# A gated linear-attention kernel with a rational MLP: its token groups split in two halves, each half's 64 rows of v stacked with the running state

## The chip, the cores and the metric

The kernel runs on one core of one Trainium2 chip. The metric is the device time of one execution in microseconds. Three runs of the kernel before gave 537.37, 537.48 and 537.78; the median is 537.48.

## The reference, cut to what matters

There are 4 batches x 8 heads, 768 tokens, head size 48. Attention is a recurrence along the tokens, and its output feeds an MLP whose activation is a quotient of polynomials:

```python
for t in range(S):
    state = alpha[:, :, t, :, None] * state + np.einsum('bhd,bhe->bhde', k[:, :, t], v[:, :, t])
    y[:, :, t] = np.einsum('bhd,bhde->bhe', q[:, :, t], state)
x = y.transpose(0, 2, 1, 3).reshape(3072, 384)
h = x @ w_in                                   # 384 -> 2048
P = a[0] + a[1]*h + a[2]*h**2 + a[3]*h**3
Q = 1 + abs(b[0])*abs(h) + abs(b[1])*h**2
out = (P / (Q + 1e-6)) @ w_out                 # 2048 -> 384
```

The weights, `a` and `b` come as 64-bit floats; the kernel joins the two words of each weight into one 32-bit float on the chip.

## The kernel before, in words

**Groups.** The 3072 tokens are cut into 24 *groups* of 128 tokens, 0 to 23, six for each batch. Within a group the recurrence is done in matrix form. Products of alpha towards the group's end (`suffix`) and from its start (`prefix`) are two scans on VectorE; k is multiplied by the one (`mult_k`), q by the other (`mult_q`), mostly on GpSimd. Of the 128 partitions, each pair of heads holds the first head's 48 dimensions in rows 0 to 47 and the second's in rows 64 to 111.

Then TensorE makes the scores k.q of the group (`sc_mm`, L505: 8 products of 128 columns, K = 48, two heads at a time in the two halves of the rows). ScalarE copies all eight heads' scores out (`sc_evac`), GpSimd zeroes the part above the diagonal (`sc_mask`). TensorE turns k into rows of tokens (`k_turn`, L523) and ScalarE copies that (`k_evac`). `attn_mm` holds three sorts of products: state times q (L547, 12 products of 128 columns and 32 output rows), v times scores (L547, 16 of the same shape), and k times v for the next state (L566, 16 products of 48 columns and 32 output rows). A 32-bit product is two records in the trace, so these are 16 records of L505, 24 + 32 of L547 and 32 of L566. `decay` (GpSimd) multiplies the state by the group's total of alpha, which `totals` makes; `kv_add` (VectorE) adds the new part. The first group of a batch (0, 6, 12, 18) has no state products, the last (5, 11, 17, 23) has no turn of k and no new state.

`x_hi` (ScalarE) and `x_lo` (VectorE) copy the group's output as a sum of two shorter floats for the MLP.

**Units.** The MLP is 96 *units* of 512 hidden values x tokens. Units 0 to 9 are plain 32-bit products (L643, L656). Units 10 to 95 are *wide*: 9 products of 512 columns in (L670) and 9 out (L689; L683 in the last super-block of tokens), with ten elementwise steps between on ScalarE, VectorE and GpSimd (t1, ah, q1, qm, t2, t3, ars, sq, p, t, g, gh, gl). Sixteen units use the tokens of four groups.

**What sets the order.** Every step is an `add` call with its engine, its prerequisites and sometimes a second engine (`alt`). A list packed into the string `ORDER` says in which order the steps are issued and which of them go to their second engine. Each engine runs its own steps strictly in that order. All DMAs of inputs go through SyncE's one queue in that order too; `raw_qk[0]` is the only buffer for k and q of groups 4 to 23, so the loads of group g wait for the transpose `tqk` of group g - 1.

**PSUM.** Scores take banks 4 and 5, the turned k then bank 4, the output y bank 4, the new state part bank 5. The constant that the scans read as a floor lies from group 4 on in bank 5, where every group's scores overwrite it: `set_floor` writes it again for each group, and the scores of group g have to wait for `prefix` of g + 1.

**Start.** `prime` is a small ScalarE instruction (function Copy) and stands late in the order.

## Time and profile before

| | |
|---|---|
| profiled execution, its own time | 537.53 us (span 535.8) |
| median of the runs | 537.48 us (537.37 to 537.78) |
| TensorE busy | 517.1 us, 97% |
| VectorE busy | 480.7 us, 90%, 716 instructions |
| ScalarE busy | 430.2 us, 80%, 730 instructions |
| GpSimd busy | 392.4 us, 73%, 387 instructions |
| DMA | 57.46 MB, 107 GB/s on average |

Busy time is the time in which at least one of the engine's instructions was under way. An instruction of VectorE or ScalarE is recorded a little longer than it holds the engine: the next one starts before the record ends. Engines are abbreviated PE (TensorE), PEld (its weight loads), DVE (VectorE), ACT (ScalarE), POOL (GpSimd), SPq (SyncE's DMA queue).

Three stretches are used below: the opening up to 129.7 us, where wide unit 16 begins; the middle up to 455.2 us, where unit 80 begins; and the close up to 535.8 us. Units are counted by nine L670 records each from the first at 93.99 us.

### The profile page before, as it was taken

The numbers are of one execution on the slowest core, as the hardware profiler recorded it, in microseconds if no ns is written. First come the engines' busy times: TensorE is split into PE (matmuls) and PEld (weight loads), VectorE is DVE, ScalarE is ACT, GpSimd is POOL, SyncE is SP. The second block draws the span as 40 slices with busy tenths as digits, with TensorE's granted clock in tenths as the row PEclk, the third lists the DMA queues.
The fourth block names the chain that finished last, engine by engine and source line by source line (L and its number), as shares of the span: only waits on it lengthen the run. The fifth ranks groups of instructions, "written<-read, shape, count | busy, mean of one in ns | idle before, by whom it ended". The sixth has DMA issues, their size and how long they took to land.

```text
span 535.8 us, 11861 instructions
## 1 busy us (share of the span) xinstructions
PE 517.1 (97%) x4342; PEld 428.1 (80%) x4342; DVE 480.7 (90%) x716; ACT 430.2 (80%) x730; POOL 392.4 (73%) x387
## 2 busy tenths in 40 slices
PE   8878997999999999999999999999999999999996
PEld 7777886888788788888778878878888887889986
DVE  3998988999998999999979989999999997898885
ACT  3699988899988977788868777777778876787983
POOL 2436557697998988996676888759888765687673
PEclk9999999999999999999999999999999999999999
DMA  9988875454555353545324524342632341020301
GB/s 246 260 249 219 214 229 116 116 140 113 128 140 117 92 127 71 104 96 109 92 68 87 112 73 94 97 87 59 128 95 55 88 83 18 1 40 1 59 1 62
DMA packets 146174, 57.46 MB, mean 107 GB/s; under 512 B 133056, under 2 KB 138688, under 8 KB 146112
## 3 DMA queue, kind: packets, MB, share of 16 engines
q1 hardware_dynamic: 145824, 56.27, 43.7%
q8 instruction: 35, 0.57, 0.5%
q10 hardware_dynamic: 288, 0.39, 0.2%
q14 instruction: 27, 0.22, 0.1%
HBM read 47.98 MB, written 4.72 MB: 98 GB/s over the span
## 4 chain that ended last, share of the span: by engine, by line
PE 70%; SPq 7%; DMA 7%; DVE 6%; POOL 4%; ACT 3%; issue 2%; DVEq 0%; POOLq 0%; ACTq 0%
PE ps L670 29%; PE ps L689 23%; PE ps L683 6%; PE ps L547 5%; SPq L402 4%; PE ps L505 3%; DMA wo_words<-in_moe_w_out_dram 2%; DMA raw_a<-in_alpha_dram 2%; PE ps L656 1%; SPq L409 1%; DMA tv<-in_v_dram 1%; POOL gh_gl L778 1%; PE ps L523 1%; PE ps L566 1%; DVE t L748 1%
## 5 line engine op out<-in xcount | busy, mean ns | idle before, releaser
L670 PE MATMUL ps<-x,wi 128*128 128x512 f32 x774 | 209.1, 396 | 3.7 <-DVE t L771 3.7
L689 PE MATMUL ps<-gh_gl,wo 128*128 128x512 f32 x630 | 176.5, 400 | 0.1
L670 PEld LDWEIGHTS ps<-x,wi 128*128 128x128 f32 x774 | 143.8, 188 | 36.1 <-ACT ah L725 3.0
L737 POOL TENSOR_TENSOR qm<-qm,ah 128x512 f32<-128x512 f32 x96 | 124.2, 1295 | 24.7 <-ACT qm L734 14.7
L689 PEld LDWEIGHTS ps<-gh_gl,wo 128*128 128x128 f32 x630 | 115.5, 188 | 27.6 <-DVE parts L704 0.5
L778 POOL TENSOR_TENSOR gh_gl<-t,gh_gl 128x512 fp32r<-128x512 f32 x74 | 96.2, 1301 | 16.4 <-ACT gh_gl L774 6.3
L728 ACT ACTIVATE t<-ps,coef 128x512 f32<-128x512 f32 x96 | 74.5, 776 | 21.2 <-PE ps L670 12.8
L755 ACT ACTIVATE ps<-qm,one_eps 128x512 f32<-128x512 f32 x96 | 66.3, 691 | 20.5 <-POOL qm L737 11.9
L732 POOL TENSOR_SCALAR qm<-ah,bab 128x512 f32<-128x512 f32 x62 | 47.8, 771 | 47.4 <-ACT ah L725 22.5
L762 DVE SCALAR_TENSOR_TENSOR t<-t,coef,ps 128x512 f32<-128x512 f32 x96 | 71.0, 739 | 12.6 <-ACT ps L758 11.7
L748 DVE TENSOR_TENSOR t<-t,ps 128x512 f32<-128x512 f32 x96 | 65.1, 678 | 11.3 <-ACT t L728 5.6
L752 DVE SCALAR_TENSOR_TENSOR t<-t,coef,ps 128x512 f32<-128x512 f32 x96 | 71.3, 744 | 2.5 <-ACT ah L725 0.7
L725 ACT ACTIVATE ah<-ps 128x512 f32<-128x512 f32 x96 | 57.0, 593 | 17.7 <-PE ps L670 12.0
L771 DVE SCALAR_TENSOR_TENSOR t<-ps,t 128x512 f32<-128x512 f32 x96 | 66.1, 688 | 1.9
L765 DVE SCALAR_TENSOR_TENSOR ps<-qm,ps 128x512 f32<-128x512 f32 x96 | 66.0, 688 | 0.0
L774 ACT ACTIVATE gh_gl<-t 128x512 fp32r<-128x512 f32 x86 | 53.7, 628 | 9.2 <-DVE t L771 7.3
L758 ACT ACTIVATE ps<-ps 128x512 f32<-128x512 f32 x96 | 56.1, 585 | 2.0
L488 POOL TENSOR_TENSOR tqk<-tqk,tg 128x512 f32<-128x512 f32 x21 | 27.2, 1294 | 13.4 <-DVE tg L461 7.7
L491 POOL TENSOR_TENSOR tqk<-tqk,fp 128x512 f32<-128x512 f32 x21 | 27.2, 1295 | 12.6 <-DVE wo_words L274 5.0
L516 POOL TENSOR_SCALAR_AFFINE_SELECT sc<-sc 128x1024 f32<-128x1024 f32 x24 | 26.2, 1092 | 13.2 <-ACT sc L512 4.0
L461 DVE TENSOR_TENSOR_SCAN tg<-ta,ps 128x528 f32<-128x528 f32 x24 | 29.8, 1244 | 6.5 <-ACT ta L445 6.5
L683 PE MATMUL ps<-wo,gh_gl 128*128 128x384 f32 x180 | 35.5, 337 | 0.0
(117 smaller groups left out, 723.0 us busy)
## 6 DMA issues: line engine op xcount, KB each, us to landing
raw_a<-in_alpha_dram SPq DMA_DIRECT2D x160, 48.0 KB, 2.1
raw_qk<-in_k_dram SPq DMA_DIRECT2D x160, 48.0 KB, 2.1
raw_qk<-in_q_dram SPq DMA_DIRECT2D x160, 48.0 KB, 2.1
wi_words<-in_moe_w_in_dram SPq DMA_DIRECT2D x8, 768.0 KB, 6.9
wo_words<-in_moe_w_out_dram SPq DMA_DIRECT2D x8, 768.0 KB, 7.0
tv<-in_v_dram SPq DMA_DIRECT2D x24, 192.0 KB, 3.2
wr<-in_alpha_dram SPq DMA_DIRECT2D x18, 256.0 KB, 3.0
out_dram<-parts SPq DMA_DIRECT2D x60, 64.0 KB, 2.3
```

The source lines that it names most:

```text
L670: nc.tensor.matmul(h_of(u), w(key)[:, kt * FU + f % FU, :], x[:, kt, xp, :], start=(n == 0), stop=(n == len(todo) - 1),)
L683: nc.tensor.matmul(bank(T_BANKS[tt], DM), g[:, tt * P : (tt + 1) * P], w(("o", f // FU))[:, f % FU, :], start=(f == 0 and first_w), stop=( ...
L689: nc.tensor.matmul(bank(O_BANKS[dt]), w(("o", f // FU))[:, f % FU, dt * P : (dt + 1) * P], g, start=(f == 0 and first_w), stop=(f == NF - ...
L728: nc.scalar.activation(buf(s, "t1", u), h_of(u), AF.Identity, bias=a2, scale=a3)
L737: nc.gpsimd.tensor_tensor(buf(s, "qm", u), buf(s, "qm", u), buf(s, "ah", u), op=ALU.mult)
L748: nc.vector.tensor_tensor(t, t, h_of(u), op=ALU.mult)
L752: nc.vector.scalar_tensor_tensor(t, t, a1, h_of(u), op0=ALU.add, op1=ALU.mult)
L755: nc.scalar.activation(h_of(u), buf(s, "qm", u), AF.Abs_reciprocal_sqrt, bias=one_eps)
L762: nc.vector.scalar_tensor_tensor(t, t, a0, h_of(u), op0=ALU.add, op1=ALU.mult)
L765: nc.vector.scalar_tensor_tensor(h_of(u), buf(s, "qm", u), 1.0 + 1e-6, h_of(u), op0=ALU.add, op1=ALU.mult)
L771: nc.vector.scalar_tensor_tensor(t, h_of(u), 2.0, t, op0=ALU.subtract, op1=ALU.mult, reverse0=True)
L778: eng.tensor_tensor(buf(s, "gl", u).rearrange("p a b -> p (a b)"), buf(s, "t1", u), gh, op=ALU.subtract)
```

## The change

1. Each group is cut in two halves of 64 tokens. Scores are made only within a half: 16 products of 64 columns, K = 48, 64 output rows; the four quadrants of the array are used in turn.
2. A new tile `sv` holds, for each half, 64 rows of v and, in the other 64 rows, the state that the half starts from. One product per head part and half (32 of 64 columns, 32 output rows, K = 128) gives v times scores plus state times q. `TURN` rotates them over the four column groups.
3. For that, scores and q must stand in one tile: `q_side` copies 48-row pieces of q to the other rows, into k's place in `tqk`; `sc_evac` (two per group) writes the scores into q's and k's rows; `sc_mask` runs twice on half the data. The tile `sc` is gone.
4. k times v (`kv_mm`) is a step of its own, with 64-row operands; the state is brought forward twice per group (`kv_mid`, `kv_add`), each as two VectorE instructions of 48 partitions x 192. `decay` is two instructions as well, or a memset in a batch's first group. `totals` becomes a copy of four columns. k is turned in every group.
5. A further buffer for loads of k and q is used by odd groups in turn with the first; v is loaded by two DMAs per group; v has 2 buffers for 3, `fp` 1 for 2.
6. The floor is written once, to a column that nothing overwrites. `prime` uses the function Abs_reciprocal_sqrt, and ScalarE's first steps wait for it.
7. `ORDER` is new.

The core of the diff (the string of `ORDER` and the step list are cut):

```diff
 NQ = 3
+NFP = 1
+NV = 2
...
+    raw_qk += ring("raw_odd", 1, [P, RAW + LINE])
...
+    CH = C // 2
+    sv = ring("sv", NV, [P, 2, H, DP])
+    st_s = work.tile([P, H, D], F32, name="st_s")
...
     def sc_mm(g):
         for a in range(NPAIR):
-            for j in range(2):
-                r = slice(DP * j, DP * j + D)
-                nc.tensor.matmul(
-                    bank(SCB + j)[:, a * C : (a + 1) * C], tk[g % NQ][r, a, :], tq[g % NQ][r, a, :],
+            for c in range(2):
+                for j in range(2):
+                    r = slice(DP * j, DP * j + D)
+                    t = slice(CH * c, CH * (c + 1))
+                    nc.tensor.matmul(
+                        bank(SCB + j)[CH * c : CH * (c + 1), CH * a : CH * (a + 1)],
+                        tk[g % NQ][r, a, t], tq[g % NQ][r, a, t], start=True, stop=True, skip_group_check=True,
...
+    def q_side(eng, g):
+        t = tqk[g % NQ]
+        for c in range(2):
+            o, x = t[toks(1 - c), 1, :, toks(c)], t[toks(c), 0, :, toks(c)]
...
+    def kv_mm(g):
+        kt = kts[g % NSC]
+        for a in range(NPAIR):
+            for j in range(2):
+                for c in range(1 if last(g) else 2):
+                    nc.tensor.matmul(
+                        bank(SCB + c)[toks(j), KV0 + D * a : KV0 + D * (a + 1)],
+                        kt[toks(c), a * KW + DP * j : a * KW + DP * (j + 1)],
+                        sv[g % NV][toks(c), c, 2 * a + j, 0:D], start=True, stop=True, skip_group_check=True,
...
     def attn_mm(g):
+        for c in range(2):
+            w = sv[g % NV][:, c].rearrange("p h w -> p (h w)")
+            for h, x in TURN:
...
+                nc.tensor.matmul(
+                    y[r : r + 32, o : o + CH], w[:, w0 : w0 + 32], tqk[g % NQ][:, int(j == c), a, toks(c)],
+                    start=r not in begun, stop=True, skip_group_check=True,
...
+    def kv_mid(g):
+        for j in range(2):
+            if first(g):
+                nc.vector.tensor_copy(state_of(g, 1)[:, j::2], kv_of(0, j))
+            else:
+                nc.vector.tensor_tensor(state_of(g, 1)[:, j::2], state_of(g, 0)[:, j::2], kv_of(0, j), op=ALU.add)
...
     def kv_add(g):
+        for j in range(2):
+            nc.vector.tensor_tensor(st_s[rows_of(1), j::2], state_of(g, 1)[:, j::2], kv_of(1, j), op=ALU.add)
...
+    add("prime", "ACT", 1.5, nc.scalar.activation, (first_act, one_eps, AF.Abs_reciprocal_sqrt), ["one_eps"])
...
+        if g == G3:
+            add("fl", "DVE", 0.17, set_floor, (), ...
```

The two packed orders, unpacked, differ in these counts of steps (before/after; one step of km, kv or qc after is two instructions; km is `kv_mid`, kv `kv_add`, qc `q_side`, se `sc_evac`, ke `k_evac`, d `decay`, fl `set_floor`; sign, hi, abs and lo are steps on the weights). Groups 8 to 23 and units 16 to 79 lie in the middle stretch in both.

| engine | opening (before unit 16) | middle (unit 16 to 80) | close |
|---|---|---|---|
| VectorE | km 0/8, kv 7/7, sign 5/1, lo 1/0, q 1/3, k 1/0, d 1/0, qc 0/1, se 0/1, tot 0/3, gl 0/1, tqk 4/5, ta 6/5, pre 9/8 | km 0/16, kv 13/13, gl 8/0, k 2/0, q 2/1, d 1/0, qc 0/1, se 0/2, tot 2/3, pre 15/16, ta 14/15, tqk 16/15 | gl 4/6 |
| ScalarE | sign 11/15, qc 0/7, se 8/15, ke 7/8, hi 9/10, ah 15/16, abs 16/15, fl 5/0, tot 0/3 | qc 0/15, se 16/30, ke 13/16, q1 24/29, gu 28/31, fl 14/0, tot 0/11 | q1 1/4, gu 8/5 |
| GpSimd | sm 8/16, d 5/7, k 7/9, lo 7/9, q 7/5, tot 7/0, abs 0/1 | sm 16/32, d 13/16, gl 56/64, k 14/15, q 14/15, q1 40/35, tot 11/0 | gl 15/13, q1 16/12 |
| TensorE | kv_mm 0/8, k_turn 7/8 | kv_mm 0/16, k_turn 13/16, out steps of three products 188/192 | out steps 58/54 |

## Rows read from the trace of the kernel before

**Rows 1.** Windows of the opening, middle and close: length, then each engine's busy time.
```profile
core 0: us, PE busy (x) PEld busy (x) DVE busy (x) ACT busy (x) POOL busy (x), PEclk, DMA share, GB/s
0.00:129.70 129.70, 117.08 (x1254) 100.45 (x1255) 112.70 (x166) 109.28 (x160) 77.90 (x102) 0.99 0.74 196
129.70:455.20 325.50, 323.54 (x2714) 259.77 (x2713) 302.64 (x452) 260.67 (x465) 261.14 (x238) 1.00 0.41 92
455.20:535.80 80.60, 76.49 (x378) 67.83 (x376) 65.33 (x100) 60.28 (x108) 53.35 (x48) 1.00 0.12 27
```

**Rows 2.** The same view, of parts of the opening and after it.
```profile
0.00:20.00 20.00, 15.85 (x186) 15.16 (x187) 11.34 (x17) 9.20 (x16) 8.02 (x37) 1.00 0.90 236
...
20.00:95.00 75.00, 66.53 (x708) 57.04 (x707) 67.45 (x100) 67.36 (x91) 41.37 (x42) 0.98 0.78 213
95.00:150.00 55.00, 55.00 (x542) 44.67 (x541) 53.70 (x80) 51.70 (x84) 48.41 (x39) 1.00 0.51 122
```

**Rows 3.** Chain that ended last, 0 to 130 us: start, length, what.
```profile
34.93 1.28 ACT L755
...
52.03 11.92 DMA raw_a<-in_alpha_dram
...
72.98 9.15 DMA wo_words<-in_moe_w_out_dram
```

**Rows 4.** Timeline of TensorE, products of one group among the units: start, length, what.
```profile
407.41 1.16 PE L505 MATMUL ps<-tqk 48*128 48x128 f32 x16
408.50 0.95 PE L689 MATMUL ps<-gh_gl,wo 128*128 128x512 f32 x3
...
412.78 0.55 PE L523 MATMUL ps<-ident,tqk 112*128 112x112 f32 x4
413.10 1.64 PE L689 MATMUL ps<-gh_gl,wo 128*128 128x512 f32 x6
...
418.18 0.86 PE L547 MATMUL ps<-tqk,st_d 128*32 128x128 f32 x24
418.86 1.06 PE L547 MATMUL ps<-sc,tv 128*32 128x128 f32 x32
419.73 0.52 PE L566 MATMUL ps<-tv,kt 128*32 128x48 f32 x32
420.18 1.43 PE L670 MATMUL ps<-x,wi 128*128 128x512 f32 x5
```

**Rows 5.** Timeline of VectorE, the same group's state and its neighbours.
```profile
420.88 0.55 DVE L576 TENSOR_TENSOR st_s<-st_d,ps 128x384 f32<-128x384 f32 x1
421.34 0.74 DVE L762 SCALAR_TENSOR_TENSOR t<-t,coef,ps 128x512 f32<-128x512 f32 x1
```

**Rows 6.** Instructions by line and shape: operation, count, busy us, mean ns, idle before.
```profile
L479 DVE TENSOR_TENSOR tot<-tg,halves 128x8 f32<-128x8 f32 x2 | 0.3, 160 | 0.0
...
L778 DVE TENSOR_TENSOR gh_gl<-t,gh_gl 128x512 fp32r<-128x512 f32 x12 | 8.2, 684 | 1.0 <-issue 0.7 <-POOL sc L516 0.2
...
L512 ACT ACTIVATE sc<-ps 128x1024 f32<-128x1024 f32 x24 | 24.8, 1032 | 5.3 <-PE ps L505 5.3
...
L725 ACT ACTIVATE ah<-ps 128x512 f32<-128x512 f32 x96 | 57.0, 593 | 17.7 <-PE ps L670 12.0 <-DVE t L752 3.8 <-DVE t L748 1.4
...
L445 ACT ACTIVATE tqk<-ps 128x256 f32<-128x256 f32 x4 | 1.5, 406 | 0.3 <-PE ps L426 0.3
```

**Rows 7.** Timeline of ScalarE: its first instruction, and a sign step with what follows.
```profile
7.14 1.28 ACT L445 ACT_TABLE_LOAD   x1 [7.14 <-PE ps L426]
...
31.40 1.99 ACT L278 ACTIVATE wo_words<-wo_words 128x768 f16<-128x768 f32 x1
33.10 1.15 ACT L512 ACTIVATE sc<-ps 128x1024 f32<-128x1024 f32 x1
```

**Rows 8.** Waits of the DMA queue, 130 to 455 us: who for whom, total, times, longest.
```profile
SPq L402 <- DVE tqk L458: 55.6, 14, 8.2
```

**Rows 9.** Waits of all engines, 0 to 130 us.
```profile
DVE tqk L458 <- DMA raw_a<-in_alpha_dram: 2.2, 1, 2.2
```

**Rows 10.** The v loads' issue on the DMA queue: ns min, median, max.
```profile
L449 SPq DMA_DIRECT2D tv<-in_v_dram x24: 385/422/1467, 6.3 to 423.3; - x24
```

More of the change, by code (lines that the diff above doesn't have):

```diff
@@ L950, in tile_gla_then_rational_mlp @@
         add(("set", "ta", s), "POOL", 0.1, set_ta, (s,))
-    for s in range(3):
+    add(("set", "k", 2), "POOL", 0.1, set_raw, (2, "k"))
+    for s in range(NV):
         add(("set", "v", s), "POOL", 0.3, set_v, (s,))
-    add("halves", "POOL", 0.4, set_halves)
-    add("consts", "DVE", 0.8, set_consts, (), ["halves"])
+    add("consts", "DVE", 0.8, set_consts)
     add("set_st", "POOL", 0.6, set_st)
@@ L999, in tile_gla_then_rational_mlp @@
                     add(("cp", m, nm, par, cc), "ACT", 0.6 if par is None else 0.38, copy_nat, (m, nm, par, cc),
-                        [("tn", m, nm, x) for x in range(2) if par in (None, x)] + into[nm])
+                        [("tn", m, nm, x) for x in range(2) if par in (None, x)] + into[nm] + ["prime"])
                 ready[nm] = [("cp", m, nm, par, cc) for par in pairs]
@@ L1015, in tile_gla_then_rational_mlp @@
         add(("k", g), "POOL", 1.3, mult_k, (g,), [("suf", g)] + ready["k"], alt=("DVE", 0.72, True))
         add(("q", g), "POOL", 1.3, mult_q, (g,), [("pre", g)] + ready["q"], alt=("DVE", 0.69, True))
-        if not first(g):
-            add(("tot", g), "POOL", 0.24, totals, (g,), [("suf", g), "halves", "consts", ("d", g - NQ)], alt=("DVE", 0.16, True))
-        add(("v", g), "SP", DMA, load_v, (g,), [("set", "v", g % 3), ("am", g - 3)], kb=1.05)
+        for c in range(2):
+            add(("sv", g, c), "SP", DMA, load_sv, (g, c), [("set", "v", g % NV), ("am", g - NV), ("vk", g - NV)], kb=0.9)
@@ L1025, in tile_gla_then_rational_mlp @@
-        if not last(g):
-            add(("kt", g), "PE", 0.38, k_turn, (g,), [("se", g), ("k", g)], lat=0.13)
-            add(("ke", g), "ACT", 0.55, k_evac, (g,), [("kt", g), ("am", g - NSC), "set_st"])
-        if not first(g):
-            add(("d", g), "POOL", 0.86, decay, (g,), [("kv", g - 1), ("am", g - 1), ("tot", g), "set_st"], alt=("DVE", 0.56, True))
-        add(("am", g), "PE", SV[1] if not (first(g) or last(g)) else SV[1] - (SV[2] if first(g) else SV[3]), attn_mm, (g,),
-            [("sm", g), ("d", g), ("ke", g), ("v", g), "set_st", ("xl", g - 1), ("xh", g - 1)], lat=0.13)
@@ L1032, in tile_gla_then_rational_mlp @@
-        if not last(g):
-            add(("kv", g), "DVE", 0.54, kv_add, (g,), [("am", g), ("d", g)])
+        was = [("xh", g - 1), ("xl", g - 1), ("km", g - 1), ("kv", g - 1), ("se", g - 1, 0), ("se", g - 1, 1)]
+        add(("kt", g), "PE", 0.38, k_turn, (g,), [("k", g)] + was + near, lat=0.13)
+        add(("ke", g), "ACT", 0.55, k_evac, (g,), [("kt", g), ("vk", g - NSC), "set_st"])
+        add(("s", g), "PE", SV[0], sc_mm, (g,), [("k", g), ("q", g), ("ke", g)] + was + near, lat=0.13)
+        add(("vk", g), "PE", SV[3], kv_mm, (g,), [("ke", g), ("sv", g, 0), ("sv", g, 1)] + was, lat=0.13)
@@ new lines, in tile_gla_then_rational_mlp @@
+        add(("qc", g), "ACT", 0.72, q_side, (g,), [("s", g), ("kt", g)], alt=("DVE", 0.8, True))
+        for c in range(2):
+            add(("se", g, c), "ACT", 0.67, sc_evac, (g, c), [("s", g), ("qc", g)], alt=("DVE", 0.69, False))
+            add(("sm", g, c), "POOL", 0.66, sc_mask, (g, c), [("se", g, c)])
+        if g:
+            if not first(g):
+                add(("tot", g), "ACT", 0.18, totals, (g,), [("suf", g), ("d", g - 2)], alt=("DVE", 0.16, False))
+            add(("d", g), "POOL", 1.1, decay, (g,), [("suf", g), ("tot", g), ("kv", g - 1), ("km", g - 1), ("am", g - NV), ("set", "v", g % NV)], alt=("DVE", 0.72, True))
@@ L1034, in tile_gla_then_rational_mlp @@
+        add(("km", g), "DVE", 0.71, kv_mid, (g,), [("vk", g), ("d", g), ("am", g - NV), ("set", "v", g % NV)])
+        if not last(g):
+            add(("kv", g), "DVE", 0.71, kv_add, (g,), [("vk", g), ("km", g), ("d", g)])
+        add(("am", g), "PE", SV[1], attn_mm, (g,), [("sm", g, 0), ("sm", g, 1), ("s", g), ("qc", g), ("d", g), ("km", g), ("sv", g, 0), ("sv", g, 1), ("xl", g - 1), ("xh", g - 1)], lat=0.13)
     for g in range(NGC):
```

301 lines of the change are left out of this document (140 added, 161 removed).

## The prediction, made before the changed kernel ran

> **What bounds the kernel now.** I read the busy time by windows first. In the middle stretch TensorE is busy 323.5 of 325.5 us and VectorE 302.6, or 93%; ScalarE and GpSimd stand at 80% [rows 1]. So TensorE ends every wait there, with VectorE close behind: whatever shortens TensorE by more than some 5% hands the bound to VectorE. In the opening no engine is full from 20 to 95 us: TensorE 66.5, VectorE 67.5 and ScalarE 67.4 of 75 us, DMA 78% [rows 2]. The chain of waits says why: it runs through transfers that queue behind each other, 11.92 us for a load of alpha and 9.15 for a weight block, and through ScalarE's table load of 1.28 [rows 3]. In the close TensorE has 76.5 of 80.6 [rows 1], and no group work is left.
>
> The timeline of one group gives its price on TensorE, from start to next start [rows 4]: scores 1.09 us for 16 records (68 ns each), the turn of k 0.32, state and v products 1.55 for 56 records (27.7 ns each), k times v 0.45 for 32 (14.1 ns each). That is 3.41 for a group inside a batch; 2.73 for a batch's first group (24 records of 28.3 ns fewer) and 2.64 for its last (without the turn and k times v).
>
> **The change, part by part.**
>
> *TensorE.* The output becomes 64 records of 64 columns, 32 rows out, K = 128. The nearest rows are the records of 48 columns (14.1 ns) and of 128 columns (27.7 ns) of the same 32-row shape [rows 4]. On the line between them 64 columns cost 16.8 ns; by columns alone 13.9. So 0.89 to 1.07 us; I take 1.0. The scores become 32 records of half the columns and half the output rows. If half a record costs half of 68 ns, 34, they take 1.09 as before; if a second pair of quadrants runs beside the first, 17 ns, or 0.55. The bounds are 0.45 (14.1 ns each) and 1.09; I take 0.55, because the 32-row products, with the same 128 columns and one of four column groups each, follow at 27.7 ns where the scores need 68. k times v stays at 32 records of 48 columns; its weights are 64 columns wide for 32, so 0.45 to 0.90, I take 0.5 (half in a batch's last group). The turn stays at 0.32 and is now made in every group. Sum 2.37, and 2.12 in a last group. Saved: 1.04 inside a batch, 0.36 in a first group, 0.52 in a last. The middle holds 11, 2 and 3 of these: 11.4 + 0.7 + 1.6 = 13.7 us. Against it the new order puts four more out steps of three products, 0.70 each by the three of L689 in [rows 4] before their overlap with the next, into the middle, 2.8, which the close loses. TensorE's middle load: 323.5 - 13.7 + 2.8 = 312.6. With the bounds of the three prices a group inside a batch costs 2.11 to 3.38, so the load lies between about 309 and 326.
>
> A rule speaks against this part. What the row shows: 14.1 ns from record to record with 48 columns and 32 output rows [rows 4]. The Trainium skill, page "TensorE: Matmul & The Clock Gate", section "Wait — 56ns, not 53.3ns?", says that start to start never falls below about 25 ns however few columns a matmul has. By it the new group would cost 0.32 + 64 x 25 + 32 x 25 + 32 x 25 ns = 3.5 us, more than now, and the middle would gain nothing on TensorE. The trace is against it where column groups take turns, and it decides for me; what is left of the idea is the second rival.
>
> *VectorE.* `kv_mid` and `kv_add` are two instructions each of 192 elements where one of 384 stood. That one is recorded with 0.55 us, and the next starts 0.46 after it [rows 5]; one of 8 elements is recorded with 0.16 [rows 6]. Between them 192 elements give 0.35, less the 0.09 that overlaps, 0.27: 0.54 a pair. Bounds: 0.30 a pair (mostly fixed cost, nearer to the 8 elements) and 0.92 (each like the 384). In the middle 16 + 13 pairs replace 13 instructions: 29 x 0.54 - 13 x 0.46 = +9.7 (+2.7 to +20.7). The order takes 8 gl of 0.68 [rows 6], 0.6 net, from VectorE: -4.8; three k and q multiplies and a decay go too, -2.2; one qc and two se come, +1.9; steps of groups that fall on the other side of a mark, +1.3. Sum +5.9: 308.5. VectorE cannot run without gaps, since its steps wait for ScalarE and GpSimd in turn; the fullest long row is 53.7 of 55, or 97.6% [rows 2]. 308.5 / 0.976 = 316. TensorE with its present 2 us of idle needs 314.6. Two engines this near to full delay each other; I take 318 for the middle, **-7.5 us**.
>
> *ScalarE.* qc is 30 copies of 256 columns in the middle, recorded with 0.41 each [rows 6], 0.31 net; se turns 16 of 1.03 into 30 of about 0.59, the price of 512 columns [rows 6], which comes to nothing; q1, ke, tot and guards add some 7. 260.7 + 17 = 278 of 318: covered, as long as VectorE or TensorE is the slower. *GpSimd* gets 8 more gl and two-part decays, some +12: 273 of 318, covered too.
>
> *The opening* is where ScalarE's extra work is not covered. Four sign steps move there from VectorE, at 1.70 from start to next start [rows 7]: +6.8. qc: 7 x 2 x 0.31 = +4.3. The rest of its steps: +0.7. Against it both table loads leave the busy part, the first because `prime` now brings it into the 7.14 us in which ScalarE waits for the first transpose [rows 7], the second because the same table then serves [rows 3]: -2.6. So 109.3 + 9.2 = 118.5, of which some 8.5 fit before 20 us, where it is busy 9.20 now, loads included [rows 2]. The other 110 at 97.6% take 112.7, and the opening ends at 132.7 where it ends at 129.7: **+3 us**. VectorE (+2) and TensorE (-6.6) are not late there. Bounds: -3 (the time that TensorE and the chain give back) and +13 (the third rival).
>
> *Loads.* The second buffer ends the wait of k's and q's loads for the transpose of the group before, 55.6 us over the middle [rows 8]. All of it lies beside a full TensorE, so I count nothing. In the opening the transpose waited 2.2 us for alpha's load [rows 9], which stays single: 0, at best -2.2. Twice as many loads of v, each issued in 0.42 [rows 10], add 10 us to a queue that has those 55 to spare; behind each in the queue stand weights and alpha, and in the opening they could come up to 0.4 later each.
>
> *Floor, tot, waits.* That the floor is written once takes 19 small ScalarE steps away and frees the scores of a group from the scan of the next; no engine shows idle for that. New waits: the output now waits for qc, two se, two masks and `kv_mid`. The order puts about ten pieces of unit work between scores and output where four or five stood, so TensorE has 9 us of cover; without it a group would cost it 1 to 2 us.
>
> *Close.* Four out steps fewer: **-2.8**.
>
> **Sum.** +3 - 7.5 - 2.8 = -7.3. The profiled execution took 537.53 (span 535.8 and 1.7 around it), 0.05 over the median of the runs; 537.5 - 7.3 = **530.2 us**, 1.4% less.
>
> **Rivals.**
> 1. *TensorE stays the bound.* VectorE's small instructions cost little (0.30 a pair gives 301.5, or 309 at 97.6%) and TensorE's saving comes through whole: middle 314.6, opening -3. 537.5 - 10.9 - 3 - 2.8 = 521. For it: TensorE at 99.4% in the middle; against it: VectorE's 93% before anything is added.
> 2. *Small products cost by the piece.* Quadrants don't run beside each other and a record has a floor near 25 to 34 ns. A group costs about 3.5; the middle gains nothing, loses some 4 us in its first and last groups, and the opening's +3 comes on top, less 1: 543. For it: the 68 ns of the scores, where 27.7 is reached elsewhere; against it: the 14.1 ns.
> 3. *ScalarE in the opening.* It is the one engine with 9 us more to do in a stretch in which DMA, not it, sets the pace. If after 20 us it gets no further than its 89.8% of now [rows 2], 110 us take 122.5, because qc and se stand in front of the weights' sign steps and units start later, and the opening ends at 142.5: +13. Then 537.5 + 13 - 10.3 = 540. It decides from +10.3 on, that is from a busy share under 92% after 20 us. For it: VectorE, ScalarE and TensorE are all near 90% there without any being full, so chains of waits, not loads, set the pace; against it: the TensorE work there falls by 6.6.
> 4. *The parts cancel.* TensorE's prices come out in the middle of their bounds, VectorE's near the upper one (327 for the middle): 537 to 539.
>
> **How the numbers follow.** Forecast 0.50, with 524 to 535 as its own range; first rival 0.19; second 0.09; third 0.14; fourth 0.08. About 0.2%, 1.1 us, is what a measurement tells from no change. Faster: the forecast and the first rival, 0.69, and a little of the others, less the forecast's edge: 0.70. Same: most of the fourth, 0.08. Slower 0.22. The range of 8 in 10 reaches from the first rival's time, 520, to the second's, 542.
>
> **What would show it.** Right: records of the output about 16 ns apart, scores under 0.7 us, VectorE over 96% of a middle near 318 with TensorE showing idle time released by VectorE, an opening near 133 with ScalarE over 95% after 20 us, one table load before 7 us. Wrong: output records 25 ns apart, the new VectorE instructions far from 0.35, or a middle shorter than VectorE's load as computed; an opening that ends before 129 or after 137.

## The result: 0.8% slower, where 1.4% faster was predicted

The changed kernel takes 540.96 us (median of 14 runs, 538.30 to 547.02), the kernel before 536.95 beside it (14 runs, 535.27 to 539.42). The ratio is 1.0077, with a 95% interval of 1.0052 to 1.0102: +4.0 us, where the forecast was 530.2 in a range of 520 to 542. The run of 547.02, over 1.5% above the fastest, is left out of the ratio. The profiled execution took 543.5 (span 541.8), 2.5 above the median. Windows of the changed kernel, cut at the same units as [rows 1], then a part of its opening as in [rows 2]; columns as there:

```profile
0.00:140.70 140.70, 122.47 (x1513) 101.30 (x1514) 119.99 (x189) 122.41 (x181) 87.54 (x105) 0.93 0.70 182
140.70:463.00 322.30, 317.56 (x3217) 249.61 (x3217) 311.83 (x492) 285.80 (x522) 276.96 (x265) 1.00 0.44 93
463.00:541.80 78.80, 73.74 (x366) 65.62 (x364) 65.01 (x101) 58.94 (x103) 48.19 (x43) 1.00 0.11 25
...
20.00:95.00 75.00, 62.78 (x822) 52.65 (x812) 68.09 (x107) 70.34 (x99) 42.46 (x44) 0.91 0.75 198
```

| us | predicted | changed kernel, profiled | the same with TensorE's clock held (e5, below) |
|---|---|---|---|
| opening | +3 | +11.0 | +4.7 |
| middle | -7.5 | -3.2 | -3.4 |
| close | -2.8 | -1.8 | -2.0 |
| sum | -7.3 | +6.0 | -0.7 |

The middle gained less than half of what was forecast and the opening lost several times as much. The column to see first is PEclk: 0.93 over the opening, where it was 0.99.

*What TensorE's clock did.* Windows of the changed kernel, chosen by the granted clock:

```profile
16.00:22.80 6.80, 6.53 (x112) 5.59 (x113) 5.84 (x11) 5.59 (x8) 1.99 (x3) 0.50 1.11 325
22.80:53.40 30.60, 24.34 (x424) 21.56 (x423) 28.08 (x45) 29.60 (x47) 17.82 (x20) 1.00 0.85 222
53.50:60.30 6.80, 5.92 (x51) 3.92 (x53) 6.51 (x12) 6.67 (x9) 4.28 (x6) 0.50 0.97 281
91.10:94.40 3.30, 3.30 (x30) 2.29 (x34) 3.14 (x7) 2.56 (x3) 3.30 (x3) 0.50 0.59 160
94.60:125.00 30.40, 28.62 (x389) 23.15 (x378) 28.32 (x44) 28.83 (x48) 25.68 (x23) 1.00 0.53 126
125.30:128.50 3.20, 3.20 (x9) 2.42 (x9) 3.16 (x6) 2.30 (x5) 3.20 (x3) 0.50 0.56 110
```

Four stretches, 20 us in all, run at 0.50, the 1.2 GHz level; before, one of 3.4 us does. Three of the four follow a piece of 1.8 to 2.5 us in which TensorE stood still. Timeline of TensorE around the second, and of ScalarE, for which it waited (start, length, what; idle before):

```profile
47.93 1.46 PE L668 MATMUL ps<-x_whole,wi_words 128*128 128x256 f32 x6
49.22 0.55 PE L537 MATMUL ps<-ident,tqk 112*128 112x112 f32 x4
52.26 0.69 PE L504 MATMUL ps<-tqk 48*64 48x64 f32 x32 [2.49 <-ACT kt L540]
52.94 2.38 PE L668 MATMUL ps<-x_whole,wi_words 128*128 128x256 f32 x6
56.20 1.11 PE L568 MATMUL ps<-sv,kt 64*64 64x48 f32 x32 [0.88 <-ACT tqk L525]
57.24 2.93 PE L668 MATMUL ps<-x_whole,wi_words 128*128 128x256 f32 x6
```

```profile
48.70 1.92 ACT L282 ACTIVATE wo_words<-wo_words 128x768 f16<-128x768 f32 x1
50.37 0.93 ACT L270 ACTIVATE wr<-wo_words 128x768 f32<-128x768 f32 x1
51.20 0.58 ACT L750 ACTIVATE ah<-ps 128x512 f32<-128x512 f32 x1
51.67 0.53 ACT L540 ACTIVATE kt<-ps 128x448 f32<-128x448 f32 x1
```

The same six records of L668 take 1.46 us at 47.93 and 2.93 at 57.24. The wait is one that the change made: scores and turned k share a bank, and the turn now stands ahead of the scores, so the scores (L504) wait until ScalarE has copied the turned k out (L540). ScalarE works in order, and a sign step (L282, 1.92), an abs step and an `ah` stand in front of that copy.

*TensorE's prices* came out near the forecast. Timeline of TensorE, groups among the units (compare [rows 4]):

```profile
166.88 1.10 PE L586 MATMUL ps<-tqk,sv 128*32 128x64 f32 x64
167.91 0.96 PE L714 MATMUL ps<-gh_gl,wo 128*128 128x512 f32 x3
...
410.85 0.55 PE L537 MATMUL ps<-ident,tqk 112*128 112x112 f32 x4
411.17 0.94 PE L714 MATMUL ps<-gh_gl,wo 128*128 128x512 f32 x3
...
415.49 0.68 PE L568 MATMUL ps<-sv,kt 64*64 64x48 f32 x32
415.99 0.66 PE L504 MATMUL ps<-tqk 48*64 48x64 f32 x32
416.58 0.95 PE L714 MATMUL ps<-gh_gl,wo 128*128 128x512 f32 x3
```

From start to next start: output 1.03 for 64 records (16.1 ns each), turn 0.32, k times v 0.50 (15.6 ns), scores 0.59 (18.4 ns): 2.44 for a group, forecast 2.37, before 3.41. The sum over all groups, which fell by less, is in the part on why the prediction was wrong.

*VectorE's did not.* Lines of the middle, grouped by shape (count, busy us, mean ns), and the timeline of VectorE in one group:

```profile
L597 DVE TENSOR_TENSOR sv<-sv,ps 48x192 f32<-48x192 f32 x28 | 9.9, 352 | 0.8
...
L601 DVE TENSOR_TENSOR st_s<-sv,ps 48x192 f32<-48x192 f32 x26 | 9.2, 352 | 0.6
```

```profile
416.93 0.18 DVE L471 RECIPROCAL ta<-tg 128x4 f32<-128x4 f32 x1
417.01 0.66 DVE L773 TENSOR_TENSOR t<-t,ps 128x512 f32<-128x512 f32 x1
417.70 0.72 DVE L597 TENSOR_TENSOR sv<-sv,ps 48x192 f32<-48x192 f32 x2
418.45 0.75 DVE L777 SCALAR_TENSOR_TENSOR t<-t,coef,ps 128x512 f32<-128x512 f32 x1
419.12 0.74 DVE L787 SCALAR_TENSOR_TENSOR t<-t,coef,ps 128x512 f32<-128x512 f32 x1
```

A record is 0.35 long, as forecast, but nothing overlaps it: the pair begins at 417.70 and the next instruction at 418.45, 0.75 later, where the 512-element instruction behind it (0.75 long) gives way after 0.67. The sum had 0.54 for a pair. Shortness is not the reason: the RECIPROCAL of 128 x 4 (0.18 long) gives way after 0.08. What sets the pair apart is that it covers 48 of the 128 partitions, and the instruction in front of it doesn't give way early either (417.01 to 417.70 for a record of 0.66). ScalarE does the same with the q copies on 64 partitions, two of 0.42 each, with the next instruction 0.89 after the first one's start:

```profile
416.68 0.86 ACT L514 ACTIVATE tqk<-tqk 64x256 f32<-64x256 f32 x2 [0.46 <-PE ps L504]
417.57 0.69 ACT L780 ACTIVATE ps<-qm,one_eps 128x512 f32<-128x512 f32 x1
```

Counted over the whole changed kernel, where the next instruction waits for no semaphore: between two instructions of 128 partitions the second starts before the first one's record ends in 45 of 46 cases on VectorE and in 101 of 102 on ScalarE; where one of the two covers 48 or 64 partitions, in 1 of 46 and in 2 of 23. So it is for instructions of 128 partitions alone that the next one starts before the record ends, and [rows 5] and [rows 7], which have only such, could not price the new ones. Whether the number of partitions counts or where they begin was not tested.

### The profile page after: what moved, and what is told of

Same layout as the page of the kernel before. It is cut to its first block, busy times and chain, and to the rows that moved or that the text cites. A ratio compares the mean times of both kernels' runs of the same rounds, so it can differ in the third digit from the quotient of the medians.

```text
span 541.8 us, 13660 instructions
## 1 busy us (share of the span) xinstructions
PE 513.8 (95%) x5094; PEld 416.5 (77%) x5094; DVE 496.8 (92%) x779; ACT 467.1 (86%) x804; POOL 412.7 (76%) x411
## 4 chain that ended last, share of the span: by engine, by line
PE 57%; DVE 13%; ACT 12%; DMA 6%; issue 4%; POOL 4%; SPq 3%; DVEq 0%; POOLq 0%; ACTq 0%
PE ps L695 21%; PE ps L714 17%; PE ps L708 6%; PE ps L681 3%; PE ps L586 3%; SPq L401 2%; DMA raw_a<-in_alpha_dram 2%; PE ps L668 2%; ACT ps L780 2%; DMA raw_qk<-in_q_dram 2%; DVE ps L790 2%; DVE t L787 2%; DVE t L773 1%; PE ps L568 1%; PE ps L504 1%
## 5 line engine op out<-in xcount | busy, mean ns | idle before, releaser
L695 PE MATMUL ps<-x,wi 128*128 128x512 f32 x774 | 201.3, 399 | 4.8 <-DVE t L796 4.7
L714 PE MATMUL ps<-gh_gl,wo 128*128 128x512 f32 x630 | 168.6, 401 | 0.2 <-ACT gh_gl L799 0.2
L803 POOL TENSOR_TENSOR gh_gl<-t,gh_gl 128x512 fp32r<-128x512 f32 x79 | 102.5, 1299 | 16.0 <-ACT gh_gl L799 9.7
L773 DVE TENSOR_TENSOR t<-t,ps 128x512 f32<-128x512 f32 x96 | 65.2, 679 | 10.8 <-ACT t L753 9.1
L750 ACT ACTIVATE ah<-ps 128x512 f32<-128x512 f32 x96 | 57.1, 595 | 11.8 <-PE ps L695 11.6
L757 POOL TENSOR_SCALAR qm<-ah,bab 128x512 f32<-128x512 f32 x54 | 42.1, 779 | 26.0 <-ACT ah L750 10.9
L531 POOL TENSOR_SCALAR_AFFINE_SELECT tqk<-tqk 64x512 f32<-64x512 f32 x48 | 32.5, 676 | 14.2 <-DVE wi_words L278 4.0
L483 POOL TENSOR_TENSOR tqk<-tqk,tg 128x512 f32<-128x512 f32 x24 | 30.9, 1288 | 10.0 <-ACT tqk L444 6.4
L759 ACT ACTIVATE qm<-ah,bab 128x512 f32<-128x512 f32 x42 | 34.2, 814 | 1.7 <-DVE ps L790 1.3
L708 PE MATMUL ps<-wo,gh_gl 128*128 128x384 f32 x180 | 33.8, 338 | 0.0
```

The source lines that it names most:

```text
L695: nc.tensor.matmul(h_of(u), w(key)[:, kt * FU + f % FU, :], x[:, kt, xp, :], start=(n == 0), stop=(n == len(todo) - 1),)
L708: nc.tensor.matmul(bank(T_BANKS[tt], DM), g[:, tt * P : (tt + 1) * P], w(("o", f // FU))[:, f % FU, :], start=(f == 0 and first_w), stop=( ...
L714: nc.tensor.matmul(bank(O_BANKS[dt]), w(("o", f // FU))[:, f % FU, dt * P : (dt + 1) * P], g, start=(f == 0 and first_w), stop=(f == NF - ...
L773: nc.vector.tensor_tensor(t, t, h_of(u), op=ALU.mult)
L803: eng.tensor_tensor(buf(s, "gl", u).rearrange("p a b -> p (a b)"), buf(s, "t1", u), gh, op=ALU.subtract)
```

## The experiments

Between two of them, differences of the ratios to before are compared, times 536 us. In the expectations A is the theory that the loads of ScalarE and VectorE set the pace; other letters hold only where they are explained.

### TensorE's clock

**e2_q_first**: the order in which the first DMAs are issued, as before.

```diff
-a0 k0 v0.0 coef q0 v0.1 w(i1) a1 w(i0) q1 k1 ...
+a0 k0 q0 a1 v0.0 v0.1 w(i1) w(i0) q1 k1 coef ...
```

> The changed kernel with the start of the DMA queue as in the kernel before: q's first block ahead of v and of the coefficients, alpha's second block next. Theory B: the first unit starts 4 to 6 us earlier and the time falls by 3 to 6 us, to 535 to 538. Theories A and C: the gain at the start is lost again by 60 us, the time within 1.5 us of the changed kernel.

**e3_clock_filler**: 16 products that add zero, put where TensorE stood still (scores of group 3, k times v of groups 3 and 4, wide unit 14).

```diff
+    def filler(n):
+        for _ in range(n):
+            nc.tensor.matmul(bank(6, 256), ident, naught, start=False, stop=False, skip_group_check=True)
```

> The changed kernel with 16 filler products (256 columns of zeros added to an output accumulator, some 0.43 us each) at the four places of the opening where TensorE stood idle for 0.9 to 2.5 us before its clock fell (scores and k times v of group 3, k times v of group 4, unit 14). Nothing else changes and no other engine gets less work. Theory C: three of the four stretches at 1.2 GHz go, mean granted clock 0.993 or more for 0.981 to 0.99, time 3 to 6 us less. Theory A: the clock rises, but ScalarE still sets the pace: less than 1.5 us.

**e5_start_and_filler**: both, and four more fillers at unit 4.

```diff
+        if u == 4 and ff == 0:   # plain_out
+            filler(4)
```

> The changed kernel with both the DMA order at the start of the second experiment and the filler products of the third, and four more of them where unit 4's first output products waited 1.6 to 1.9 us. If the late start and the clock are two separate losses, their gains add: 1 to 2 us under either alone, 0 to 1 us under the kernel before. If the start's gain was itself only fewer falls of the clock, or the other engines set the pace of the opening after 40 us: the same as the third experiment within 0.7 us.

Measured: e2 537.86 (ratio 1.0026 [1.0006, 1.0047]), e3 537.62 (1.0017 [0.9998, 1.0035]), e5 537.34 (1.0020 [1.0000, 1.0039]). Either edit takes back some 3 us of the 4; both together no more. e3, which changes nothing but the fillers, is the clean test: its theory C had 3 to 6 us, and 3.2 came. e2 mixes two causes: its time is the one that theory B had, but the first unit starts 2.2 us earlier (26.5 for 28.7), not 4 to 6, and its profile has three stretches of 3.4 us at the lower clock in the opening in place of 20 us. In e3 one of 3.4 us is left in the opening, in e5 none: the granted clock is 1.00 up to the end of the span. Windows of e5:

```profile
0.00:134.40 134.40, 122.56 (x1554) 102.43 (x1554) 120.16 (x189) 122.04 (x181) 87.81 (x106) 1.00 0.71 187
134.40:456.50 322.10, 317.27 (x3217) 249.56 (x3216) 311.76 (x492) 285.07 (x522) 277.43 (x265) 1.00 0.43 95
456.50:535.10 78.60, 73.73 (x366) 65.63 (x364) 65.00 (x101) 58.81 (x103) 48.30 (x43) 1.00 0.11 25
20.00:95.00 75.00, 68.79 (x837) 58.63 (x835) 72.00 (x113) 73.99 (x106) 45.15 (x46) 1.00 0.76 201
```

With the clock held, ScalarE is busy 73.99 of 75 us (98.7%) from 20 to 95 us, where it had 70.34; the opening ends at 134.4. Its instructions are as many (181) and as long in both.

The sharpest pair came unplanned. e4 (below) has the changed kernel's code in the opening, unaltered, and its profiled execution opens in 134.8 us, not 140.7. TensorE in the changed kernel, then the same code and the same idle piece in e4:

```profile
90.39 0.67 PE L568 MATMUL ps<-sv,kt 64*64 64x48 f32 x30 [2.41 <-DVE tg L462]
91.00 2.88 PE L681 MATMUL ps<-t,wo_words 128*128 128x256 f32 x6
93.81 1.40 PE L586 MATMUL ps<-tqk,sv 128*32 128x64 f32 x64
```

```profile
87.19 0.68 PE L566 MATMUL ps<-sv,kt 64*64 64x48 f32 x30 [2.38 <-DVE tg L460]
87.80 1.56 PE L679 MATMUL ps<-t,wo_words 128*128 128x256 f32 x6
89.29 1.10 PE L584 MATMUL ps<-tqk,sv 128*32 128x64 f32 x64
```

After 2.4 us of idle time the clock fell in the one (2.88 us for six records) and not in the other (1.56). So the idle pieces expose the kernel to the fall; whether it comes differs from execution to execution. That fits with the scatter: over the 13 runs in the ratio, 0.01 of mean granted clock goes with 3.8 us of time (correlation -0.82; 538.30 at 0.995, 544.11 at 0.979). e3's mean clock is higher by 0.01, and its time lower by 3.2 us.

**e12_before_filler**: fillers at the two long idle pieces of the kernel before.

```diff
+        if g == 2:            # attn_mm
+            filler(5)
...
+        if u == 10 and part == 0:   # wide_in
+            filler(5)
```

> The kernel of before with filler products at its own two long idle pieces of TensorE (ahead of the attention of group 2 at 35.6 us and of wide unit 10 at 91.3 us). If the lower clock after the first piece costs before about as much as one such stretch costs the changed kernel (theory: the clock is a cost of either), before gains 0.5 to 2 us: 534 to 535.5. If VectorE and ScalarE have the slack to take it back before unit 16 (rival), it stays at 535.5 to 536.5, and the clock matters to the changed kernel alone.

536.88 (1.0000 [0.9981, 1.0019]): the kernel before gains nothing. In its profile the stretch at 38 us is gone, but one of 6.8 us stands at 16 us instead, so it is a weak test of what the clock costs before. Its first plain unit starts some 3.5 us later for that (25.4 for 21.8), and its opening still ends at 129.4.

### The middle

**e4_km_twice**: `kv_mid` twice for groups 8 to 23, 32 more VectorE instructions of 0.35 us.

```diff
-        for j in range(2):
+        for j in (0, 1, 0, 1) if g >= 8 else (0, 1):
```

> The changed kernel with kv_mid issued twice for groups 8 to 23 (the same values again): 32 more VectorE instructions of 192 elements, 0.27 us each, 8.6 us in all, nearly all in the middle stretch. If VectorE bounds the middle, as the prediction said: 6 to 9 us longer. If TensorE still bounds it: less than 2 us.

**e10_no_km_middle**: on e5, without `kv_mid` there.

```diff
-        for j in range(2):
+        for j in range(2) if g < 8 else ():
```

> The same version (start order of before, filler products) without the update of the state by k times v in groups 8 to 23 (32 VectorE instructions of 0.35 us, 11.3 us; that part of the computation is missing). If VectorE's load sets the pace of the middle (theory A), the middle falls from 322 to between 312 and 316, ScalarE and TensorE close behind then limiting it, and the time by 6 to 9 us, to 528 to 531. If TensorE still sets it (rival: TensorE stays the bound), the middle falls by less than 2 us and the time stays at 535.5 to 537.5.

**e15_late_moves**: on e5, six late steps (the expectation says seven) go from VectorE to ScalarE.

```diff
-tot 20, tot 21, tot 23, se (20, 1), se (23, 0), qc 23: VectorE
+tot 20, tot 21, tot 23, se (20, 1), se (23, 0), qc 23: ScalarE
```

> The same version with seven late steps moved from VectorE to ScalarE: tot of groups 20, 21 and 23, two score copies and one copy of q (about 2.5 us of VectorE). If VectorE's load is what units 64 to 80 wait for (theory A), the time falls by 1 to 2.5 us, to 535 to 536.3; if TensorE is the bound there (as the run without the state's update in the middle says), by 0 to 1: 536.3 to 537.5.

Windows of the middle, of e4, e10 and e15:

```profile
134.80:465.60 330.80, 320.45 (x3218) 249.20 (x3217) 322.68 (x525) 286.29 (x523) 277.07 (x266) 1.00 0.42 92
```

```profile
134.50:456.50 322.00, 318.34 (x3217) 250.80 (x3216) 301.17 (x460) 284.42 (x522) 276.53 (x265) 0.99 0.43 95
```

```profile
133.80:454.00 320.20, 316.72 (x3218) 249.91 (x3217) 307.28 (x485) 287.35 (x529) 276.97 (x265) 1.00 0.43 95
```

e4: 548.23 (1.0218 [1.0181, 1.0255]), 7.6 us over the changed kernel, as expected for VectorE as the bound; its middle is 8.7 us longer than e5's for 10.9 us more of VectorE. e10: 534.85 (0.9971 [0.9958, 0.9984]); 10.6 us less of VectorE bring 2.6 us by the ratios, none in the profiled execution, which had one stretch of 3.4 us at 1.2 GHz in the middle (some 1.7 us). The expected 6 to 9 didn't come: A falls in its plain form. e15: 536.60 (1.0015 [0.9998, 1.0032]); 0.3 us by the ratios, less than can be told, though its profiled middle is 1.9 shorter. What holds the middle near 320 once VectorE is eased is, by its busy share, TensorE: 316.72 of 320.20, 98.9%; no run eased TensorE to show it. The two engines stand within 6 us of each other, and easing one shows the other at once.

### The opening

**e1_sign_back**: the sign steps on the engines of before, five on VectorE instead of one.

```diff
-sign o0: VectorE; sign i0, i1, i2, i4, o3: ScalarE
+sign o0: ScalarE; sign i0, i1, i2, i4, o3: VectorE
```

> The changed kernel with the sign steps on the weights on the engines that the kernel before used (blocks i0, i1, i2, i4 and o3 on VectorE, o0 on ScalarE), in the same places of the order. Theory A, ScalarE's added work makes the opening long, these steps the largest part of it (four of 1.7 us): the opening ends 3 to 5 us earlier than the 140.7 of the changed kernel, the time is 536 to 538. Theory B, the opening is late because the first transfers stand in another order (the first unit's first product at 28.7 us for 21.8): within 1 us of the changed kernel. Theory C, the falls of TensorE's clock are the loss: it gains only as far as TensorE's idle pieces of over 1.5 us go.

544.08 (1.0127 [1.0092, 1.0163]), 2.7 us slower than the changed kernel, which none of the three theories had. VectorE's load in the opening rises from 119.99 to 125.02 us there, ScalarE's falls from 122.41 to 115.36: VectorE has no room for these steps either.

**e6_km_twice_opening** and **e7_qc_twice_opening**: on e3, `kv_mid` or `q_side` twice in groups 1 to 7.

```diff
-        for j in range(2):              # e6, kv_mid
+        for j in (0, 1, 0, 1) if 1 <= g < 8 else (0, 1):
-        for c in range(2):              # e7, q_side
+        for c in (0, 1, 0, 1) if 1 <= g < 8 else (0, 1):
```

> The third experiment's kernel (with fillers) with kv_mid issued twice for groups 1 to 7: 14 more VectorE instructions, 4.9 us of VectorE in the opening, the same values. If VectorE sets the pace of the opening: 3 to 5 us longer than the third experiment. If ScalarE or the transfers do: 0 to 1.5 us.

> The third experiment's kernel with q_side issued twice for groups 1 to 7: 14 more copies on ScalarE of 0.42, 5.9 us of ScalarE in the opening, the same values. If ScalarE sets the pace of the opening (third rival): 4 to 6 us longer than the third experiment. If VectorE or the transfers do: 0 to 2 us.

**e11_no_qc_opening** and **e13_no_qc_no_km_opening**: on e5, the same steps left out, `q_side` alone and then both.

```diff
-        for c in range(2):              # e11 and e13, q_side
+        for c in () if 1 <= g < 8 else range(2):
-        for j in range(2):              # e13, kv_mid
+        for j in () if 1 <= g < 8 else (0, 1):
```

> The same version without the copies that carry q into k's place in groups 1 to 7 (14 ScalarE instructions of 0.42 us, 5.9 us; that part of the computation is missing). If ScalarE's load sets the pace of the opening (theory A as predicted), the opening falls from 134.4 by 3 to 5 us and the time to 532 to 534. If VectorE is the one that is full there, or both alike, the opening falls by 0 to 2 us and the time stays at 535.5 to 537.5; that doubling either engine's steps cost 1:1 would fit with both.

> The version with the start order of before and the filler products (537.3 us, opening 134.4), without the copies of q and without the first update of the state in groups 1 to 7: ScalarE has 5.9 us less to do in the opening and VectorE 4.9 (those parts of the computation are missing). If ScalarE and VectorE together set the pace there (theory A: with the copies alone left out 2.2 us came back of 5.9), the opening falls by 5 to 6 us, to 128.5 to 129.5, and the time to 531 to 532.5. If what is left of the opening's loss is in loads and in TensorE's waits (rival C), it falls by the same 2.5 us as without the copies alone, to about 132, and the time stays near 535.

Opening windows of e6, e7, e11 and e13:

```profile
0.00:139.40 139.40, 122.02 (x1545) 101.28 (x1546) 124.87 (x203) 122.29 (x181) 88.42 (x106) 1.00 0.71 185
```

```profile
0.00:140.00 140.00, 123.66 (x1545) 103.09 (x1546) 120.24 (x189) 127.43 (x195) 88.70 (x106) 0.98 0.69 181
```

```profile
0.00:131.90 131.90, 122.57 (x1554) 103.43 (x1554) 120.30 (x189) 116.64 (x167) 88.19 (x106) 0.99 0.73 191
```

```profile
0.00:131.70 131.70, 122.94 (x1554) 104.27 (x1555) 117.61 (x175) 116.16 (x167) 89.10 (x106) 0.99 0.74 191
```

The same of e11 and e13, from 20 us on:

```profile
20.00:131.90 111.90, 107.74 (x1335) 89.77 (x1333) 108.76 (x171) 105.14 (x153) 80.70 (x77) 0.98 0.69 179
```

```profile
20.00:131.70 111.70, 108.11 (x1353) 90.54 (x1343) 106.78 (x158) 105.12 (x153) 81.63 (x77) 0.98 0.71 180
```

e6: 542.19 (1.0107 [1.0080, 1.0134]), +4.8 us on e3 for 4.9 us of VectorE. e7: 543.50 (1.0121 [1.0096, 1.0146]), +5.6 for 5.9 of ScalarE, two stretches at the lower clock in its opening included. e11: 535.12 (0.9979 [0.9959, 0.9998]), -2.2 us for 5.9. e13: 534.21 (0.9971 [0.9952, 0.9991]), -2.6 for 10.8. What is added to either engine costs nearly its whole length; what is taken away brings 2.2 us of the first 5.9, and the next 4.9 bring nothing that can be told from it. Theory A holds in part: with ScalarE eased in e11, VectorE is the one that is full, 108.76 of 111.90 us from 20 us on, or 97.2%, where the fullest long row of before has 97.6% [rows 2]. e13 ends its opening about where its rival C had it, but it doesn't speak against VectorE: the steps left out are 4.9 us, yet VectorE's load falls only from 120.16 in e5 to 117.61, since its other instructions are recorded 2.2 us longer in all (above all copies of totals and steps on the weights; why was not traced), and from 20 us on it is still busy 95.6% (95.4% in e5). So what keeps the opening near 131.7, 2 us over before, is VectorE as far as these rows tell; no run shows it by itself. e11 and e13 also have one stretch of 3.4 us at the lower clock each.

### Work for GpSimd

**e9_best_try**: e15 with abs steps, q of groups 2 and 23 and gl of unit 10 on GpSimd. **e16_late_and_two_early**: e15 with q of group 2 and gl of unit 10 alone. **e18_copies_to_gpsimd**: e15 with the q copies of groups 1 to 7 on GpSimd.

```diff
-abs o1, i4, o2, o3, o4: ScalarE; q 2, q 23, gl 10: VectorE
+abs o1, i4, o2, o3, o4, q 2, q 23, gl 10: GpSimd            # e9; e16: q 2 and gl 10
+        if 1 <= g < 8 and eng is nc.scalar:      # q_side
+            eng = nc.gpsimd                                  # e18
```

> The version with the start order of before and the filler products, with work moved off the engines that are full: five abs steps, q's multiply of groups 2 and 23 and gl of unit 10 from VectorE and ScalarE to GpSimd, and some small late steps between VectorE and ScalarE. If the changed kernel is bound in the opening and the middle by the load of ScalarE and VectorE (theory A), the opening loses 2 to 4 us from 134.4 and the middle 2 to 4 from 322, and the time falls from about 537.3 to 531 to 535, below before's 536. If waits in the order of the steps and not the loads set the pace (rival B), or GpSimd's steps arrive late, nothing is gained: 536 to 540.

> As the run before, and two early steps go from VectorE to GpSimd: q's multiply of group 2 and gl of unit 10 (about 1.8 us of VectorE in the opening; GpSimd is busy some 65% there). If VectorE's load sets the opening's pace (theory A), it falls by 0.5 to 1.5 us from 134.4, and the time to 534 to 535.5, under before's 536; if GpSimd, which works in order, brings them late (rival B), the opening grows by 1 to 4 us and the time is 537 to 540.

> The version with the seven late steps moved (536.6 us), and the copies that carry q into k's place in groups 1 to 7 made by GpSimd in place of ScalarE. Leaving them out brought 2.2 us. If ScalarE's load is what counts (theory A) and GpSimd, some 70% busy there, takes them beside its other work, the time falls by 1 to 2.2 us, to 534.4 to 535.6, at or under before's 535.9. If GpSimd's order makes them late, since the score copies and the output wait for them (rival B), the opening grows by 1 to 5 us: 537.5 to 541.

e9: 546.37 (1.0196 [1.0177, 1.0214]); e16: 538.18 (1.0043 [1.0025, 1.0060]); e18: 541.01 (1.0093 [1.0069, 1.0118]). e16 and e18 fall where rival B had them, e9 beyond its 540. TensorE's waits in e9 from 45 to 70 us and the window after them, and ScalarE's waits in e18 from 100 to 140 us (total, times, longest):

```profile
PE ps L676 <- DVE t L808: 3.9, 1, 3.9
```

```profile
54.90:68.50 13.60, 11.07 (x114) 8.27 (x115) 11.68 (x16) 8.04 (x11) 9.56 (x9) 0.50 0.55 157
```

```profile
ACT tqk L533 <- POOL tqk L524: 5.9, 2, 3.3
```

In e9 one wait of 3.9 us is followed by 13.6 us at 1.2 GHz. In e18 ScalarE's load falls, but its score copies (L533) wait for the q copies on GpSimd (L524), and TensorE's k times v for the score copies (3.5 us in two waits). No version that makes the whole computation beats before; the nearest are e15 and e5, within 0.2%.

### The start and the loads

**e8_prime_alone**: the kernel before with the small ScalarE instruction at the head of the order.

```diff
-nc.scalar.activation, (first_act, one_eps, AF.Copy)
+nc.scalar.activation, (first_act, one_eps, AF.Abs_reciprocal_sqrt)
```

> The kernel before with one part of the change alone: prime stands at the head of the order and uses the function Abs_reciprocal_sqrt, so that the one table is loaded while ScalarE waits for the first transpose. ScalarE loses 2.57 us of table loads after 7 us. As the prediction had it, the opening gives back 1.3 to 2.6 us of it; if ScalarE did not set the pace there before the change: less than 0.8 us.

538.12 (1.0013 [0.9987, 1.0039]): the 1.3 to 2.6 us that the prediction's step would give back lie outside the interval, so the table loads that it takes out of the opening's path are worth at most 0.7 us in the kernel before.

**e14_one_buffer** and **e17_one_buffer_in_order**: on e5, without the second buffer; in e17 the loads also stand behind the transposes.

```diff
     def raw_at(g):
-        return 2 * (g % 2)
+        return 0
```

> The same version with the second buffer for loads of k and q undone: all groups from 4 on load into the first. As the prediction has it the second buffer is worth nothing, since the wait that it ends lay beside a full TensorE: 536.5 to 538. Rival: the opening's loads (groups 4 to 7) come late without it, the transpose and with it the group waits, and 1 to 4 us are lost: 538.5 to 541.

> The second load buffer undone in the version with the start order of before and the filler products, and each of the 59 loads of k and q that stood ahead of the transpose of the group before now stands right behind it in the order. (In e14_one_buffer they had stayed ahead: there such a load overwrites the group before while it is still to be read, so that part of the input is wrong and the transposes wait for the next group's loads; its time says nothing on the buffer.) By the prediction's step on loads the second buffer is worth nothing in the middle, where the wait lay beside a full TensorE: the middle stays at 322 and the time at 536.5 to 538.5. Rival: with VectorE as full as TensorE the late transposes now show, and the middle grows by 2 to 6 us: 539 to 544.

e14 (554.06; 1.0328 [1.0301, 1.0356]) says nothing, for the reason that e17's expectation gives. e17: 578.33 (1.0779 [1.0749, 1.0808]), far beyond both expectations; its middle is 358.7 us long. Waits of the DMA queue in its middle:

```profile
SPq L405 <- DVE tqk L463: 64.6, 11, 11.4
```

That is hardly more than the 55.6 of before [rows 8], beside which TensorE was full; with the second buffer it is 8.6 (e5). The new order leans on that buffer: 59 loads had stood ahead of the transpose of the group before. How much of the 36 us is the late loads and how much the clock, 0.95 on average in e17's middle, was not separated. What the buffer would bring to the order of before was not tried.

## Why the prediction was wrong, step by step

The sign was wrong because two steps failed and the rest had too little to spare.

1. *"VectorE (+2) and TensorE (-6.6) are not late there"* (the opening) failed twice. VectorE's load there grew by 7.3 us (112.70 [rows 1] to 119.99). Only 2.9 of it is longer work by the sum of its records (125.9 to 128.8); the other 4.4 is overlap between neighbours that is gone (13.2 to 8.8), with the 30 new instructions of 48 partitions among them. So it is full, 72.00 of 75 us in e5, and e6 pays its 4.9 us whole. TensorE was late in another way: it has less to do, so it stands still, in waits that the new order of turn, scores and copies made, and then runs at 1.2 GHz. The prediction counted no such cost; [rows 2] had shown a PEclk of 0.98, and it was passed over. Worth: 3 us of the 4 in the median by e3 (6 in the profiled execution, by e5's opening).
2. *VectorE in the middle*: 0.27 net for an instruction of 192 elements, by taking over the overlap of the 384-element one, which covers 128 partitions. Not even the whole 0.35 is enough: from a pair's start to the next instruction's it is 0.77 (median of 29), and before 27 of the 29 the instruction in front loses its overlap of 0.08 too, so a pair takes some 0.85 where 0.54 were counted. VectorE's load is 311.8, not 308.5; other terms of the sum came out smaller than counted and were not traced. The rule "97.6% at most" held: 96.7% of 322.3.
3. *TensorE in the middle*: 317.6 busy, not 312.6. Summed from start to next start over all records, the groups' products take 51.4 us before and 39.8 in e5: 11.6 saved, where 13.7 were counted, k times v alone 0.60 a group where the sum had 0.5. The units' products rise by 5.1 us (272.2 to 277.3), where the four out steps more were counted at 2.8. Most of that difference: a wide product behind a group's piece or behind a short wait is followed after 0.31 to 0.34 us, where the others take 0.23, in both kernels; 65 do so in the middle of e5 and 48 before, 1.7 us. This term mattered as much as VectorE's: with VectorE 10.6 us lighter in e10 the middle still takes 322.0, some 1.7 of it by the lower clock.
4. *ScalarE in the opening* was nearly right: 118.5 us forecast, 122.0 in e5; from 20 us on 111.0 of 114.4, or 97.0%, against 110 at 97.6%. The 14 q copies are 1.8 of the difference: 0.44 from start to next start, where 0.31 were counted with the overlap of 128 partitions. Hence +4.7 with the clock held, against +3. The forecast's check (over 95%, an opening near 133) is met there and missed in the changed kernel (140.7).
5. *Close*: TensorE's load fell by 2.75, as forecast; 1.8 to 2.0 of it show.

Two slips in the prediction's sums changed little. 0.35 less 0.09 is 0.26, not 0.27, 0.6 us over 29 pairs. And the upper bound of TensorE's middle load leaves out that first and last groups would get dearer at the upper prices: 328, not 326.

So without the clock the sum is -0.7 by profiled spans and +0.2% by the medians (e5), the place of the fourth rival, "the parts cancel"; the clock adds the rest. The third rival gave 540 us, and 540.96 came, but that is luck: its opening of 142.5 was to come from ScalarE held up by order alone, and with the clock held ScalarE reaches 98.7%. The first rival (521) fell on VectorE and TensorE together. The second fell with the prices: the rule in the Trainium skill, page "TensorE: Matmul & The Clock Gate", section "Wait — 56ns, not 53.3ns?", that start to start never falls below about 25 ns, doesn't hold for these products; 64 records of the output follow each other at 16.1 ns, 32 of the scores at 18.4.

Two things stay open: the last 2 us of the opening, for which VectorE's load is the likeliest cause (e11) but not the shown one, and why the same idle piece is followed by the lower clock in one execution and not in the next. Another lead for the first: the first product of a plain unit starts at 28.7 us (26.7 in e5) where it started at 21.8, and at that point TensorE has no unit to work on, so the cover of 9 us on which the prediction counted is missing. e12 speaks against it: there the kernel before starts that product at 25.4 and ends its opening at 129.4 all the same.

## What to carry to other kernels

When a change shortens TensorE's work in a stretch that TensorE doesn't bound, ask where it will now stand still, and look for its granted clock there: the time saved comes back as idle pieces, and what follows them may run at half speed. Price a small instruction by a row of its own partitions and length, from start to next start; an overlap seen between instructions of 128 partitions doesn't carry over to one of 48 or 64, and its neighbour in front loses its own. Doubling a step tells that an engine has no slack, not that taking the step away would pay: where several engines are full together, added work costs its length and removed work brought a quarter to two fifths of it. And look at what a run without a step really took off the engine: in e13 it was half.

## What the runs showed of the hardware

An idle piece of 1.8 to 2.5 us was followed by 3.4 to 6.8 us at the 1.2 GHz level in some executions and by none in others of the same code; one of 3.9 us by 13.6 us. Twenty zero-adding products in such pieces kept the clock at 1.00 to the end of the span in the profiled execution, and at 0.996 or more on average in all 12 runs. VectorE instructions of 128 partitions give way some 0.08 us before their record ends (45 of 46 that nothing else held up), ScalarE's some 0.10 (101 of 102); next to one of 48 or 64 partitions neither does (1 of 46 and 2 of 23 do), and the next one starts 0.01 to 0.03 us after the record's end.
